# Weights in four chunks and a new instruction order in a fused scan and MLP kernel

## The chip, the core and the metric

The kernel runs on one core of a Trainium2 chip. Times are device microseconds of one execution; the figure for a kernel is the median over its runs.

## What is computed

The input is x, one sequence of 2,048 rows of 448 bf16 values. With xn the layernorm of x, the output is x + s * silu(m), where s is a complex diagonal state space model over the sequence and m a two-layer network for each row, which normalises xn again:

```
xn = layernorm(x)
s:  Bu = xn @ B_bar^T;  h[t] = Lam_bar * h[t-1] + Bu[t];  s = 2 Re(h @ C^T) + xn * Dskip
m:  layernorm(xn) @ w1 + b1  ->  gelu (tanh form)  ->  @ w2 + b2
out = x + s * silu(m)
```

w1 is 448 x 1792 and w2 1792 x 448, both bf16. B and C are 448 x 448, given as real and imaginary parts. The rest (Lambda, log_dt, Dskip, b1, b2) are vectors.

## The kernel before

**Tiling.** A block is 256 rows, laid out as 128 partitions with two rows each: `par` 0 is the even row and 1 the odd one. There are 8 blocks `x0` to `x7` and 4 groups `g` of two blocks. TensorE does nearly everything that is large; each part is one helper, and its line names it in the profile:

- `mm1` (L683) and, for group 0, `mm1_half` (L699) multiply the normalised and transposed rows `xn2T` by w1, two of the 14 column blocks of w1 a step (`j` from 0 to 6). `mm1_half` does it for one block of 256 rows at a time (`b` 0 or 1), so that work can begin with block 0 alone. ScalarE takes the gelu of each step from PSUM into `gT` (L690, L706).
- `mm2` (L714) multiplies `gT` by w2, 14 matmuls of 448 columns for each quarter of a group. VectorE adds b2 (L717, tile `b2bc`, which holds b2 on every partition), ScalarE takes a tanh (`th`, L718), VectorE forms `g_sb` (L719).
- `bu` (L613) multiplies the rows `xnT` by the transposed input matrix `BT`, in four steps a group (7 to 14 matmuls each), all into PSUM bank 4. ScalarE copies the bank into `u_sb` (L617) before the next step of `bu` may write it. `ssm` then scans along the sequence on VectorE (L638).
- `m0` (L602) and `ym` (L746, L749, L752) form the output of the state space model, with `CQ`, `CZ` and `M0` derived from C. VectorE multiplies it by `g_sb` (L755, tile t3) and adds the residual (L758), and SP stores it.
- `skip` (L730, L731) forms, for the odd rows, `xd` = xn * dbc and then `xr` = x + xd * g_sb. `dbc` is half of Dskip on every partition. It is loaded from POOL's queue and scaled by 0.5 on POOL (L338).

**Transposes and loads.** Nearly all DMAs are issued from SP's queue, in order: first x0 in two halves, w1, x1, b1 (one row of the w1 tile), B (tile `Bn`), w2, blocks 2 and 3, and C (tile `Cn`, which lies inside `gT`). Then come transposing DMAs: `xnT`, `xn2T` (for all groups but 0, whose `xn2T` comes from TensorE transposes, L379 and L437, copied by VectorE at L381 and L443), seven `BT`, each made from a `Bn` column block that VectorE finishes at L566, and four `Cr` that read all of C. `bu` step i needs BT i and 3 + i; its last step needs BT 6.

**Order.** Nothing is scheduled at run time. The helpers record 625 tasks, each with an engine, the keys it reads and the keys it writes. `emit` issues them in the order of a written list, `ORDER`. A task that the list `SECOND` names takes the second of two engines that it was given (`kb.either`). Each engine takes its instructions in that order and waits on semaphores for what a task's keys require, so an instruction that waits holds everything behind it on its engine, and a DMA that waits holds the queue.

**Chunks before.** w1 is loaded as two halves of 896 columns. Each half takes two DMAs, one for 384 of the 448 rows and one for the last 64, and a step waits for the halves that its columns lie in. w2 is loaded as two DMAs of 7 column blocks each, and `mm2` waits for both. The function `fcol` picks the columns of w1 so that block fi of a half is every seventh column, which fits the layout in which w2 is read (7 rows of w2 in a row for each partition).

Of the kernel before, what the change touches and what calls it, by code (L numbers as in the profile page):

```python
# [139 lines left out]
def dram_ap(t, offset, ap):  # L140
    return bass.AP(tensor=t.tensor, offset=offset, ap=ap)
# [4 lines left out]
ORDER = [int(k) for k in """  # L146
0 11 18 22 12 1 9 10 19 23 14 83 16 20 24 17 2 15 5 21 25 13 27 3 26 7 8 85 6 28 4 86 29 91 40 87 30 92 84 88 93 31 89 41 94 32 43 42 44 90 48 97 95
45 33 49 47 96 50 34 59 99 108 46 51 100 110 57 109 101 102 98 35 103 52 112 58 111 53 114 113 39 137 104 116 115 105 176 140 136 106 60 117 138 55 61
118 56 139 107 177 54 141 62 120 175 146 63 119 148 67 163 64 122 142 164 65 144 68 121 161 124 69 66 147 123 71 149 126 77 150 125 81 70 152 143 128
78 154 72 74 127 153 130 73 151 129 79 36 162 132 131 303 82 155 134 75 302 76 178 266 80 307 133 305 135 309 165 167 304 145 308 306 168 310 270 179  # L150
267 156 166 171 181 169 157 172 274 180 158 170 37 314 311 315 271 316 159 312 227 160 313 278 268 38 183 272 269 282 228 275 173 273 182 285 229 317
279 318 186 174 283 280 362 230 281 184 392 320 284 231 363 321 188 286 276 364 185 232 287 277 235 319 233 365 236 366 187 234 395 237 322 368 245
367 241 189 191 243 370 369 244 192 193 323 240 371 194 195 372 197 413 324 415 374 419 417 373 196 199 200 325 375 412 416 414 203 380 418 198 420
326 204 201 238 215 239 327 202 246 213 216 205 248 421 422 328 376 424 425 219 430 206 220 255 223 256 431 257 329 214 258 259 207 381 330 224 388
377 382 208 427 383 378 242 428 379 249 247 209 250 426 389 251 252 217 253 390 384 218 254 423 210 260 221 261 222 211 262 225 472 332 212 226 474
263 473 264 385 265 331 386 288 475 333 338 476 336 334 341 478 477 289 335 342 480 479 339 340 344 482 387 337 481 391 345 291 346 343 290 347 348
349 484 350 483 292 429 293 351 393 295 352 485 356 502 357 394 294 490 296 190 358 353 354 355 359 360 297 298 491 492 486 299 361 432 523 522 526
527 525 398 487 529 488 524 528 489 433 530 399 493 494 300 434 396 505 400 397 531 534 535 401 495 536 532 496 540 435 402 541 403 405 503 404 436
497 504 537 301 538 437 406 539 600 408 438 407 441 439 542 442 498 440 533 443 446 543 450 447 449 570 544 451 448 545 571 499 455 456 444 457 453
445 458 572 452 459 460 409 546 467 574 461 573 410 462 463 466 464 454 465 547 468 575 469 576 411 470 548 471 500 552 578 577 551 553 549 579 556  # L160
580 550 561 558 582 581 554 555 559 508 501 583 562 560 564 584 557 509 563 510 506 603 511 566 585 588 512 586 513 587 507 565 515 567 568 592 589
514 569 590 516 517 591 596 593 601 594 602 595 518 597 598 609 519 599 606 520 610 521 604 611 613 605 607 608 612 617 614 621 615 618 616 619 622
620 623 624
""".split()]
SECOND = [int(k) for k in """
138 141 142 143 167 171 173 197 199 217 223 284 311 318 320 393 395 396 421 422 424 425 428 503 505 506 507 532 534 535 538 541 603
""".split()]
# [11 lines left out]
def bass_recurrent_scan__ssm_conv_s5__mixer_channel_mlp__prompt_kernel(  # L179
# [18 lines left out]
    with ExitStack() as es:  # L198
# [75 lines left out]
        with nc.Block():  # L274
# [37 lines left out]

            NW1 = 2

            def ldw1(c, prio):
                w = F // NW1
                ld("sp", w1_sb[:, 0:3, c * w:(c + 1) * w],
                   dram_ap(B_w1, c * w, [[F, 128], [128 * F, 3], [1, w]]), [f"w1_{c}"], 384 * w * 2, prio, dur=0.55)
                ld("sp", w1_sb[0:64, 3, c * w:(c + 1) * w], dram_ap(B_w1, 384 * F + c * w, [[F, 64], [1, w]]),
                   [f"w1r_{c}"], 64 * w * 2, prio)  # L320

# [5 lines left out]
            ld("sp", w1_sb[64:65, 3, :], dram_ap(B_b1, 0, [[F, 1], [1, F]]), ["w1b"], 4000, S1 + 1)  # L327
            ldw1(1, S1 + 3)
            for ri, bm in enumerate((A_B_re, A_B_im)):
                ld("sp", Bn[:, ri * 3:ri * 3 + 3, D:896], dram_ap(bm, 0, [[D, 128], [128 * D, 3], [1, D]]),  # L330
                   [f"Bn{ri}"], 344000, S1 + 5, dur=0.9)
                ld("sp", Bn[ri * 64:ri * 64 + 64, 6, D:896], dram_ap(bm, 384 * D, [[D, 64], [1, D]]), [f"Bn6{ri}"], 57000, S1 + 5, dur=0.55)
            for q in range(2):
                ld("sp", w2_sb[:, q * 7:q * 7 + 7, :],
                   dram_ap(B_w2, q * 7 * 128 * D, [[7 * D, 128], [D, 7], [1, D]]), [f"w2_{q}"], 650000, S1 + 6, dur=1.7)
            ld("pool", b2bc[:], dram_ap(B_b2, 0, [[0, 128], [1, D]]), ["b2bc"], 114688, -50, reads=["sgn3"])
            ld("pool", dbc[:], dram_ap(A_Dskip, 0, [[0, 128], [1, D]]), ["dbc"], 114688, -20, reads=["b2bc"])
            pool(lambda e: e.tensor_scalar(dbc[:], dbc[:], 0.5, None, op0=ALU.mult), ["dbc"], ["dbc"], 0.8, -20)  # L338
            ldx(2, 2, S1 + 7)
# [334 lines left out]
            def fcol(fi):  # L674

                q, t = divmod(fi, 7)
                return slice(q * 896 + t, q * 896 + 896, 7)

            def mm1(g, j, prio):
                gx, gb = g % 2, g % 2  # L680
                b0 = (j % 2) * 2
                rhs = xn2T[:, gx, :, :].rearrange("p (r d) c -> p d r c", r=2)
                fns = [lambda e, k=k, d=d: e.matmul(psum[:, b0 + k, :], w1_sb[:, d, fcol(2 * j + k)],  # L683
                                                    rhs[:, d, :, :], start=(d == 0), stop=(d == 3))
                       for k in range(2) for d in range(4)]
                w = F // NW1
                cs = sorted({(2 * j * 128) // w, ((2 * j + 2) * 128 - 1) // w})
                pe(fns, [f"xmT{gx}_{b}" for b in range(2)] + [f"w1_{c}" for c in cs] + [f"w1r_{c}" for c in cs] + ["w1b"],
                   [f"ps{b0}", f"ps{b0 + 1}"], 1.75, prio)
                act(lambda e: e.activation(gT[:, gb, 2 * j:2 * j + 2, :], psum[:, b0:b0 + 2, :], ACT.Gelu_apprx_tanh),  # L690
                    [f"ps{b0}", f"ps{b0 + 1}"] + (WK + WKP if g == 1 else []), [f"gT{gb}_{2 * j + k}_{b}" for k in range(2) for b in range(2)], 1.05, prio - 70, "gelu")

            def mm1_half(j, b, k3, prio):
# [8 lines left out]
                       for k in range(2) for d in range(4)]  # L702
                w = F // NW1
                ws = sorted({(2 * j * 128) // w, ((2 * j + 2) * 128 - 1) // w})
                pe(fns, (["xmT0p0", "xmT0p1"] if b == 0 else ["xmT0_1"]) + [f"w1_{c}" for c in ws] + [f"w1r_{c}" for c in ws] + ["w1b"], [f"ps{k}" for k in banks], 0.89, prio)
# [4 lines left out]
            def mm2(g, b, par, prio):  # L710
                gb, q = g % 2, par * 2 + b
                n = (2 * g + b) * 2 + par
                gs, fb, bk = n % 8, n % 2, 5 + n % 2
                fns = [lambda e, fi=fi: e.matmul(psum[:, bk, 0:D], gT[:, gb, fi, q * 128:(q + 1) * 128], w2_sb[:, fi, :],  # L714
                                                 start=(fi == 0), stop=(fi == NF - 1)) for fi in range(NF)]
                pe(fns, [f"gT{gb}_{fi}_{b}" for fi in range(NF)] + ["w2_0", "w2_1"], [f"ps{bk}"], 2.66, prio)
                dve(lambda e: e.tensor_tensor(o2[:, fb, :], psum[:, bk, 0:D], b2bc[:], ALU.add), [f"ps{bk}", "b2bc"], [f"oo{fb}"], 0.62, prio - 76)  # L717
                act(lambda e: e.activation(th[:, fb, :], o2[:, fb, :], ACT.Tanh, scale=0.5), [f"oo{fb}"] + (WK + WKP if g == 0 else []), [f"th{fb}"], 0.58, prio - 75, "gelu")  # L718
                dve(lambda e: e.scalar_tensor_tensor(out=g_sb[:, gs, :], in0=th[:, fb, :], scalar=1.0, in1=o2[:, fb, :],  # L719
                                                     op0=ALU.add, op1=ALU.mult), [f"oo{fb}", f"th{fb}"], [f"g{gs}"], 0.6, prio - 60)  # L720
# [12 lines left out]
            def ym(g, b, par, prio):  # L733
# [9 lines left out]
                def part(c0, c1):  # L743
# [7 lines left out]
                    else:  # L751
# [5 lines left out]
                    res = xr[:, b, c0:c1] if par else x_all[:, 2 * g + b, 0, c0:c1]  # L757
                    dve(lambda e: e.tensor_tensor(o_sb[:, ob, par * D + c0:par * D + c1], t3[:, fb, c0:c1], res, ALU.add),  # L758
                        [f"t3{fb}_{c0}", f"t3{fb}_256"] + ([f"xr{b}"] if par else xk(2 * g + b)), [f"o{ob}_{par}_{c0}"], 0.1 + (0.28, 0.47)[par] * w / D, prio)
                    if last:  # L760
# [103 lines left out]
```

## Time and profile before

| | before |
|---|---|
| median of 13 runs | 161.78 us (161.08 to 164.58) |
| the profiled execution: time | 163.15 us |
| its span | 161.3 us |
| granted TensorE clock | full speed in all slices |
| TensorE busy | 151.1 us, 944 matmuls |
| VectorE, ScalarE, POOL busy | 132.7, 92.5, 56.4 us |
| DMA moved | 14.70 MB, 91 GB/s in the mean |

How to read it: a line of a group, of a timeline or of a wait names the engine, the line of the kernel and the tile written. PE is TensorE, PEld its weight loads, DVE is VectorE, ACT ScalarE, SP the engine that issues DMAs, and SPq its queue. In a timeline the first two columns are the start and the length in us, and brackets hold the idle time of the engine before the first of the instructions and what ended it. A line of waits has the total in us, the number and the longest.

### The profile page before, as it was taken

What the parts mean: (1) busy time and instruction counts of PE and PEld (TensorE: products, weight loads), DVE (VectorE), ACT (ScalarE), POOL (GpSimd) and SP (SyncE); (2) the same over time, 40 slices, a digit from 0 to 9 for tenths busy, and PEclk for the clock granted to TensorE, in tenths of its full rate; (3) what the DMA queues carried; (4) which work ended last, traced back from release to release, by engine and by line L of the source; (5) the groups of instructions that cost most, each with busy time, mean ns of one, the idle gap of its engine ahead of it and who ended that gap; (6) DMA issues with size and microseconds to landing.
All of it is one profiled execution on the core that took longest, in us unless ns stands there. A gap on an engine that the chain in (4) does not pass through costs nothing.

```text
span 161.3 us, 2700 instructions
## 1 busy us (share of the span) xinstructions
PE 151.1 (94%) x944; PEld 97.3 (60%) x944; DVE 132.7 (82%) x254; ACT 92.5 (57%) x152; POOL 56.4 (35%) x132
## 2 busy tenths in 40 slices
PE   6759999996999999999999999999999999999990
PEld 6559975664567665555565555567676665555560
DVE  5477998439799899699993999997999899896763
ACT  3757999948986894956369311343269678111100
POOL 5568928078400253210003752823046000005230
PEclk9999999999999999999999999999999999999999
DMA  4999999995882006000000802053601000010021
GB/s 95 307 303 383 273 211 182 113 195 110 155 142 100 0 0 120 14 0 0 0 0 0 228 8 55 0 145 91 122 4 57 0 4 0 0 57 0 21 92 59
DMA packets 29926, 14.70 MB, mean 91 GB/s; under 512 B 24597, under 2 KB 29593, under 8 KB 29914
## 3 DMA queue, kind: packets, MB, share of 16 engines
q1 hardware_dynamic: 29810, 14.31, 38.9%
q0 software_dynamic: 96, 0.23, 1.0%
q8 instruction: 7, 0.11, 0.3%
q14 instruction: 5, 0.04, 0.1%
q10 hardware_dynamic: 8, 0.00, 0.0%
HBM read 6.89 MB, written 1.84 MB: 54 GB/s over the span
## 4 chain that ended last, share of the span: by engine, by line
PE 73%; DVE 8%; issue 5%; DMA 5%; POOL 4%; ACT 2%; SPq 2%; POOLq 0%; DVEq 0%; ACTq 0%
PE psum L683 20%; PE psum L714 20%; PE psum L613 12%; PE psum L746 11%; DMA w_sb<-in_B_w_dram 5%; PE psum L749 4%; PE psum L602 3%; SPq L84 2%; DVE lnst L357 1%; PE psum L699 1%; POOL lnw L400 1%; DVE s_f L539 1%; POOL dbc L338 1%; DVE t L755 1%; PE psum L752 1%
## 5 line engine op out<-in xcount | busy, mean ns | idle before, releaser
L714 PE MATMUL psum<-w_sb,gT 128*128 128x448 bf16 x224 | 44.5, 352 | 0.0
L683 PE MATMUL psum<-xn2T,w_sb 128*128 128x512 bf16 x168 | 38.1, 379 | 0.0
L714 PEld LDWEIGHTS psum<-w_sb,gT 128*128 128x128 bf16 x224 | 21.8, 98 | 19.4
L683 PEld LDWEIGHTS psum<-xn2T,w_sb 128*128 128x128 bf16 x168 | 21.8, 132 | 12.9 <-issue 0.2
L690 ACT ACTIVATE gT<-psum 128x1024 bf16<-128x1024 f32 x21 | 21.5, 1023 | 11.8 <-PE psum L683 11.5
L613 PE MATMUL psum<-xnT,BT 128*128 128x256 bf16 x196 | 24.0, 273 | 1.8 <-ACT u_sb L617 1.8
L613 PEld LDWEIGHTS psum<-xnT,BT 128*128 128x128 bf16 x196 | 19.0, 98 | 7.2 <-issue 2.0
L718 ACT ACTIVATE th<-o 128x448 f32<-128x448 f32 x16 | 9.1, 573 | 20.7 <-DVE o L717 20.6
L699 PE MATMUL psum<-xn2T,w_sb 128*128 128x256 bf16 x112 | 12.8, 273 | 2.9 <-DMA w_sb<-in_B_w_dram 2.9
L719 DVE SCALAR_TENSOR_TENSOR g_sb<-th,o 128x448 bf16<-128x448 f32 x16 | 10.9, 682 | 4.7 <-ACT th L718 4.7
L755 DVE TENSOR_TENSOR t<-psum,g_sb 128x448 bf16<-128x448 f32 (+2 forms) x17 | 10.1, 591 | 5.6 <-PE psum L752 3.9
L638 DVE TENSOR_TENSOR_SCAN s_f<-cw,cur,v_sb 128x256 f32<-128x256 f32 x21 | 14.4, 735 | 0.2
L699 PEld LDWEIGHTS psum<-xn2T,w_sb 128*128 128x128 bf16 x112 | 12.1, 132 | 3.2 <-DMA w_sb<-in_B_w_dram 2.0
L730 POOL TENSOR_TENSOR xr<-xd,g_sb 128x448 f32<-128x448 bf16 x4 | 4.5, 1119 | 24.8 <-DVE g_sb L719 20.9
L421 DVE TENSOR_SCALAR xn_sb<-x_all,lnw 128x448 bf16<-128x448 bf16 x20 | 10.3, 534 | 2.6 <-POOL xd L730 2.4
L746 PE MATMUL psum<-CZ,h_sb 128*128 128x448 bf16 x56 | 11.9, 352 | 0.0
L717 DVE TENSOR_TENSOR o<-psum,b2bc 128x448 f32<-128x448 f32 x16 | 9.9, 618 | 2.4 <-PE psum L714 2.2
L617 ACT ACTIVATE u_sb<-psum 128x512 bf16<-128x512 f32 x12 | 7.1, 592 | 6.8 <-PE psum L613 6.8
L422 ACT ACTIVATE xn_sb<-x_all,lnw 128x448 bf16<-128x448 bf16 x10 | 7.5, 753 | 5.4 <-DVE xn_sb L421 4.6
L746 PE MATMUL psum<-CQ,h_sb 128*128 128x448 bf16 (+2 forms) x54 | 10.5, 332 | 0.0
L706 ACT ACTIVATE gT<-psum 128x512 bf16<-128x512 f32 x14 | 8.1, 594 | 3.8 <-PE psum L699 3.8
L357 DVE BATCH_NORM_STATS2 lnst<-x_all 128x6 f32<-128x448 bf16 x14 | 8.2, 610 | 1.8 <-DMA x_all<-in_A_x_dram 1.8
(154 smaller groups left out, 221.1 us busy)
## 6 DMA issues: line engine op xcount, KB each, us to landing
w_sb<-in_B_w_dram SPq DMA_DIRECT2D x2, 784.0 KB, 8.9
out_dram<-tmp SPq DMA_DIRECT2D x7, 224.0 KB, 2.0
w_sb<-in_B_w_dram SPq DMA_DIRECT2D x2, 672.0 KB, 6.3
x_all<-in_A_x_dram SPq DMA_DIRECT2D x3, 448.0 KB, 3.8
gT<-in_A_C_re_dram SPq DMA_DIRECT2D x1, 392.0 KB, 11.6
Bn<-in_A_B_re_dram SPq DMA_DIRECT2D x1, 336.0 KB, 8.0
Bn<-in_A_B_im_dram SPq DMA_DIRECT2D x1, 336.0 KB, 7.9
gT<-in_A_C_im_dram SPq DMA_DIRECT2D x1, 336.0 KB, 12.0
```

Of the source, the lines that this page charges most:

```text
L357: dve([lambda e, b=b, par=par, q=q: e.bn_stats(lnst[:, q, :], x_all[:, 2 * g + b, par, :])], [f"x{2 * g + b}"] + (["xmT0p1"] if (g, b) == ...
L421: on = [("dve", lambda e: e.tensor_scalar(dst, src, rs, nb, op0=ALU.mult, op1=ALU.add), 0.4, 0.12), ("act", lambda e: e.activation(dst, sr ...
L613: fns = [lambda e, r=r, m=m, d=d: e.matmul(psum[:, 4, r * NK:(r + 1) * NK], BT[:, m, d, :], xnT[:, gx, d, :], start=(d == 0), stop=(d == 6 ...
L638: dve(lambda e, i=i, ri=ri, init=init: e.tensor_tensor_scan(s_f[:, i, ri, :], col(R2, i).to_broadcast([128, NK]), v_sb[:, i, ri, :], init, ...
L683: fns = [lambda e, k=k, d=d: e.matmul(psum[:, b0 + k, :], w1_sb[:, d, fcol(2 * j + k)], rhs[:, d, :, :], start=(d == 0), stop=(d == 3)) fo ...
L690: act(lambda e: e.activation(gT[:, gb, 2 * j:2 * j + 2, :], psum[:, b0:b0 + 2, :], ACT.Gelu_apprx_tanh), [f"ps{b0}", f"ps{b0 + 1}"] + (WK ...
L699: fns = [lambda e, k=k, d=d: e.matmul(psum[:, banks[k], :].rearrange("p (r c) -> p r c", r=2)[:, :, cs], w1_sb[:, d, fcol(2 * j + k)], rhs ...
L714: fns = [lambda e, fi=fi: e.matmul(psum[:, bk, 0:D], gT[:, gb, fi, q * 128:(q + 1) * 128], w2_sb[:, fi, :], start=(fi == 0), stop=(fi == N ...
L717: dve(lambda e: e.tensor_tensor(o2[:, fb, :], psum[:, bk, 0:D], b2bc[:], ALU.add), [f"ps{bk}", "b2bc"], [f"oo{fb}"], 0.62, prio - 76)
L719: dve(lambda e: e.scalar_tensor_tensor(out=g_sb[:, gs, :], in0=th[:, fb, :], scalar=1.0, in1=o2[:, fb, :], op0=ALU.add, op1=ALU.mult), [f" ...
L746: fns = [lambda e, k=k: e.matmul(psum[:, bk, c0:c1], h_sb[:, hb, k, k0:k0 + 128], cm[:, k, c0:c1], start=(k == 0), stop=False) for k in ra ...
L755: dve(lambda e: e.tensor_tensor(t3[:, fb, c0:c1], psum[:, bk, c0:c1], g_sb[:, gs, c0:c1], ALU.mult), [f"ps{bk}", f"g{gs}"], [f"t3{fb}_{c0} ...
```

## The change

**Chunks.** w1 and w2 are cut into chunks of 4, 4, 4 and 2 column blocks (`CH`). w1 takes eight DMAs instead of four, on SP's queue, and w2 four instead of two. A row of a chunk of w1 is 1,024 bytes (512 in the last one) where it was 1,792; a partition's piece of w2 is 3,584 bytes (1,792 in the last) where it was 6,272. A step of `mm1` or `mm1_half` waits for one chunk alone, `mm2` for all four of w2. x1 still stands between the first piece of w1 and the next.

**Engines.** The scaling of dbc may be on ScalarE or VectorE instead of POOL; the new list puts it on VectorE. The last two output additions (odd rows of the last block, 256 and 192 columns) may be on VectorE or POOL; the list puts the one of 192 columns on POOL. These two no longer need each other's product.

**Order.** Both lists are new; there are 631 tasks. Of what moves: TensorE does six half blocks for block 0 before the transposes of block 1, where it did five, and one after them. In group 1 it does two steps of `mm1` where it did one between the second and third step of `bu`, and three where it did one before the last. SP issues the 64-column piece of C's imaginary part behind two xnT, four BT and the two xn2T of group 1, where it stood ahead of them all; then two BT, the four Cr, and only then the last BT. POOL loads b2bc ahead of its arithmetic on the parameters instead of behind it. VectorE does the first `xd`, and takes the statistics of blocks 2 and 3 before it finishes the second BT's input. On ScalarE the second copy of u_sb comes after four tanh and before the last xn_sb pieces of that stretch, where it came after three tanh and an xn_sb. At the end TensorE does the 192 columns before the 256.

```diff
 ORDER = [int(k) for k in """
...
 SECOND = [int(k) for k in """
...
-            NW1 = 2
+            CH = ((0, 4), (4, 4), (8, 4), (12, 2))
+            chunk = [c for c, (_, n) in enumerate(CH) for _ in range(n)]
 
             def ldw1(c, prio):
-                w = F // NW1
-                ld("sp", w1_sb[:, 0:3, c * w:(c + 1) * w],
-                   dram_ap(B_w1, c * w, [[F, 128], [128 * F, 3], [1, w]]), [f"w1_{c}"], 384 * w * 2, prio, dur=0.55)
-                ld("sp", w1_sb[0:64, 3, c * w:(c + 1) * w], dram_ap(B_w1, 384 * F + c * w, [[F, 64], [1, w]]),
-                   [f"w1r_{c}"], 64 * w * 2, prio)
+                a, w = CH[c][0] * 128, CH[c][1] * 128
+                ld("sp", w1_sb[:, 0:3, a:a + w], dram_ap(B_w1, a, [[F, 128], [128 * F, 3], [1, w]]), [f"w1_{c}"], 384 * w * 2, prio, dur=0.55)
+                ld("sp", w1_sb[0:64, 3, a:a + w], dram_ap(B_w1, 384 * F + a, [[F, 64], [1, w]]), [f"w1r_{c}"], 64 * w * 2, prio)
...
             ldw1(0, S1 + 1)
             ldx(1, 1, S1 + 2)
             ld("sp", w1_sb[64:65, 3, :], dram_ap(B_b1, 0, [[F, 1], [1, F]]), ["w1b"], 4000, S1 + 1)
-            ldw1(1, S1 + 3)
+            for c in (1, 2, 3):
+                ldw1(c, S1 + 3)
...
-            for q in range(2):
-                ld("sp", w2_sb[:, q * 7:q * 7 + 7, :],
-                   dram_ap(B_w2, q * 7 * 128 * D, [[7 * D, 128], [D, 7], [1, D]]), [f"w2_{q}"], 650000, S1 + 6, dur=1.7)
+            for c, (a, n) in enumerate(CH):
+                ld("sp", w2_sb[:, a:a + n, :], dram_ap(B_w2, a * 128 * D, [[n * D, 128], [D, n], [1, D]]), [f"w2_{c}"], 98000 * n, S1 + 6, dur=0.5 + 0.1 * n)
...
-            pool(lambda e: e.tensor_scalar(dbc[:], dbc[:], 0.5, None, op0=ALU.mult), ["dbc"], ["dbc"], 0.8, -20)
+            kb.either(("act", lambda e: e.activation(dbc[:], dbc[:], ACT.Copy, scale=0.5), 0.6, 0.2),
+                      ("dve", lambda e: e.tensor_scalar(dbc[:], dbc[:], 0.5, None, op0=ALU.mult), 0.2, 0.12), ["dbc"], ["dbc"], -20)
...
             def fcol(fi):
 
-                q, t = divmod(fi, 7)
-                return slice(q * 896 + t, q * 896 + 896, 7)
+                a, n = CH[chunk[fi]]
+                return slice(a * 128 + fi - a, (a + n) * 128, n)
...
-                w = F // NW1
-                cs = sorted({(2 * j * 128) // w, ((2 * j + 2) * 128 - 1) // w})
+                cs = [chunk[2 * j]]
...
-                pe(fns, [f"gT{gb}_{fi}_{b}" for fi in range(NF)] + ["w2_0", "w2_1"], [f"ps{bk}"], 2.66, prio)
+                pe(fns, [f"gT{gb}_{fi}_{b}" for fi in range(NF)] + [f"w2_{c}" for c in range(4)], [f"ps{bk}"], 2.66, prio)
...
-                    dve(lambda e: e.tensor_tensor(o_sb[:, ob, par * D + c0:par * D + c1], t3[:, fb, c0:c1], res, ALU.add),
-                        [f"t3{fb}_{c0}", f"t3{fb}_256"] + ([f"xr{b}"] if par else xk(2 * g + b)), [f"o{ob}_{par}_{c0}"], 0.1 + (0.28, 0.47)[par] * w / D, prio)
+                    add = lambda e: e.tensor_tensor(o_sb[:, ob, par * D + c0:par * D + c1], t3[:, fb, c0:c1], res, ALU.add)
+                    rd = [f"t3{fb}_{c0}", f"t3{fb}_256"] if c0 == 0 and not (last and par) else [f"t3{fb}_{c0}"]
+                    rd += [f"xr{b}"] if par else xk(2 * g + b)
+                    on = [("dve", add, 0.1 + (0.28, 0.47)[par] * w / D, 0.12), ("pool", add, 0.2 + 1.1 * w / D, 0.15)]
+                    if last and par:
+                        kb.either(*on, rd, [f"o{ob}_{par}_{c0}"], prio)
+                    else:
+                        dve(add, rd, [f"o{ob}_{par}_{c0}"], on[0][2], prio)
```

## The prediction

> **What bounds the kernel now.** I read the page first: busy shares, the DMA row of the slices, the chain by engine.
>
> ```profile
> PE 151.1 (94%) x944; PEld 97.3 (60%) x944; DVE 132.7 (82%) x254; ACT 92.5 (57%) x152; POOL 56.4 (35%) x132
> DMA  4999999995882006000000802053601000010021
> PE 73%; DVE 8%; issue 5%; DMA 5%; POOL 4%; ACT 2%; SPq 2%; POOLq 0%; DVEq 0%; ACTq 0%
> ```
>
> TensorE is busy 151.1 of 161.3 us. The change leaves its 944 matmuls as they are, so it can only win from the 10.2 us in which TensorE stands, and can only lose by adding to them. The DMA engines are full over the first tenths of the span (4 us a slice), idle for long stretches later. The list of waits says where TensorE stands:
>
> ```profile
> PE psum L699 <- DMA w_sb<-in_B_w_dram: 2.9, 2, 1.8
> PE psum L613 <- ACT u_sb L617: 1.8, 2, 1.4
> PE psum L777 <- POOL ident L278: 1.4, 1, 1.4
> ```
>
> Two waits for w1, two for ScalarE's copy of a PSUM bank, the start. The rest is the tail (last matmul 157.27, span 161.3). TensorE's timeline places them:
>
> ```profile
> 7.33 2.80 PE L699 MATMUL psum<-xn2T,w_sb 128*128 128x256 bf16 x24 [1.13 <-DMA w_sb<-in_B_w_dram]
> 11.89 1.93 PE L699 MATMUL psum<-xn2T,w_sb 128*128 128x256 bf16 x16 [1.75 <-DMA w_sb<-in_B_w_dram]
> ...
> 35.61 1.89 PE L683 MATMUL psum<-xn2T,w_sb 128*128 128x512 bf16 x8
> 38.95 1.69 PE L613 MATMUL psum<-xnT,BT 128*128 128x256 bf16 x14 [1.45 <-ACT u_sb L617]
> ...
> 42.69 0.94 PE L613 MATMUL psum<-xnT,BT 128*128 128x256 bf16 x7 [0.32 <-ACT u_sb L617]
> ```
>
> Behind 43 us it never stands again until the tail. So all that the change can move lies before 43 us and behind 157.
>
> **1. The start: 0.45 us won.** The first w1 matmul waits for the whole first half of w1. The DMA view of that stretch (KB, us from issue to landing) shows what follows it in the queue:
>
> ```profile
> w_sb<-in_B_w_dram SPq DMA_DIRECT2D x1, 672.0 KB, 7.4
> x_all<-in_A_x_dram SPq DMA_DIRECT2D x1, 224.0 KB, 5.2
> w_sb<-in_B_w_dram SPq DMA_DIRECT2D x1, 112.0 KB, 7.5
> ```
>
> By issue plus this time: x0 is there at 3.3, the first half (784 KB) at 7.2, x1 at 8.5, the second half at 11.7. That is 201 KB/us for the first half, and 224 for the 1008 KB behind it. A new chunk of four columns is 448 KB; at 201 it lands 2.2 us behind x0, at 5.5. Then xn2T ends last: its copies (L381) end at 6.77. TensorE starts near 6.87 instead of 7.33: 0.45 won (nothing, if the chunk lands no sooner than now).
>
> **2. The second wait: 0.9 us won.** By bytes alone x1 lands at 6.5, chunks 1, 2 and 3 at 8.5, 10.5 and 11.5. The rows of a chunk are 1,024 bytes (512 in the last), not 1,792. In the trace's packets 1,792 bytes take some 78 ns and 896 bytes 47; on the line through both, 1,024 take 52 and 512 take 34, 1.17 and 1.5 times as long a byte (an estimate). Then it is 5.9, then 6.9 for x1, and 9.3, 11.6 and 13.1. The new order runs 48 matmuls of 109 ns (six half blocks, two a chunk) before x1's transposes. It wants chunk 1 at 6.87 + 1.75 = 8.6 and chunk 2 at 10.4 or 1.75 behind the late chunk 1. Waits: 0.1 by bytes, 0.7 + 0.55 by packets. b2bc, now loaded from POOL's queue in this very stretch (112 KB, 0.5 us at that rate), may add its share; its 0.8 us on POOL lies in the 2.1 us that POOL waits for ScalarE's cw. I take 0.85 against 1.75; bounds 0.1 and 1.9. x1's own chain (8.56 to 13.55 now, 5.0 us) is ready at 11.5 to 12, before its place at 13: hidden, spare 1 us. w2's four pieces land some 1 us later than now (17.95) and are wanted at 20.6 instead of 21.96: hidden, spare 1.5.
>
> [...]
>
> **3. The wait for u_sb: 1.8 us won.** The chain of waits goes back from 38.95 to POOL:
>
> ```profile
> 27.24 0.64 POOL L84 DMA_DIRECT2D dbc<-in_A_Dskip_dram  x1
> 33.14 1.57 POOL L338 TENSOR_SCALAR dbc<-dbc 128x448 bf16<-128x448 bf16 x1 [5.26 <-DMA dbc<-in_A_Dskip_dram]
> 34.80 2.02 POOL L730 TENSOR_TENSOR xd<-xn_sb,dbc 128x448 bf16<-128x448 bf16 x2
> ```
>
> xd holds xn_sb until 35.84, VectorE's next xn_sb (L421) waits 2.4 us for that, ScalarE's xn_sb waits 3.07 for VectorE, and the copy of u_sb stands behind it in ScalarE's queue. In the new order VectorE scales dbc (the nearest row, L421, has 0.39 us for the same shape), VectorE does the first xd, and ScalarE's u_sb copy stands ahead of that xn_sb. All 1.77 us go. VectorE is not the bound at that point, but the price moves to it: it now stands if dbc lands late. dbc lands near 33.1 now; VectorE comes to it near 35, spare 1.5 to 2.
>
> **4. What is late next: 1.3 us lost.** TensorE arrives 1.35 us earlier (steps 1 and 2) at what comes by DMA. L683 needs both xn2T of the second group. Now it starts at 35.61, and the second landed at 29.82 + 5.6 = 35.4: no spare.
>
> ```profile
> xn2T<-xn_sb SPq DMA_TRANSPOSE x2, 5.5
> 28.54 4.32 SPq L83 DMA_TRANSPOSE xn2T<-xn_sb  x2
> ```
>
> (DMA view of that stretch, then SP's queue, where the second issue alone took 3.0 us.) Issue to landing was 5.5 us for these two, 3.1 for later ones; the slow pair ran beside dbc's load (28.8 to 32). In the new order they again follow two xnT and four BT. x2 and x3 land some 1 us later behind the smaller pieces, and VectorE takes their statistics before it ends the second BT's input, so the pair is issued some 0.6 us later than now, at 29.2 and 30.5. At 3.1 us they land at 33.6, TensorE wants them at 34.3: no wait. At 5.5 they land at 36: 1.7 us. The BT behind bu's second step, issued between, has the same two cases: 0, or up to 1.1 more. Bounds 0 and 2.8; dbc is still loaded at the same place, so I take nearly half, 1.3. Behind it SP has a 56 KB piece of C_im, two BT, four Cr and the last BT, some 10 us at 1.3 us each: the last BT lands near 43.5 to 45, and is wanted at 34.3 + 3.45 + 1.53 + 5.18 = 44.5 plus what was waited: no more than 0.5, within the bounds.
>
> **5. The tail: 0.25 us won.**
>
> ```profile
> 157.91 0.36 DVE L755 TENSOR_TENSOR t<-psum,g_sb 128x192 bf16<-128x192 f32 x1
> 158.30 0.36 DVE L758 TENSOR_TENSOR tmp<-t,xr 128x192 bf16<-128x192 bf16 x1
> ```
>
> Now VectorE ends 1.39 us behind the last matmul, with six operations in a row. In the new order the 192 columns come first and their addition goes to POOL; behind the last matmul stand one t and one addition of 256 columns (0.41 + 0.42 in the rows): 0.9. That wins 0.45. SP ends on 28 final waits instead of 25, at 0.065 us each: 0.2 lost.
>
> **Sum.** 161.3 - 0.45 - 0.9 - 1.8 + 1.3 - 0.25 = 159.2 of span. The profiled execution took 163.15 in all, 1.85 around its span; the median of the 13 runs, 161.78, is 1.4 below it. I take the same 2.1 us off the median: 159.7.
>
> **Rivals.** (a) dbc does not hurt the transposes, step 4 costs nothing: 158.4. For it: later transposes land in 3.1 us, and b2bc's load at 23 us slowed nothing. Against: dbc and its neighbours keep their places. (b) The wait moves: step 4 costs its 2.8, or w1 still comes as late as now; the gain of steps 1 and 2 is given back and 161.1 remains. For it: L683 has no spare now. (c) Slower: the C_im piece is now issued behind the xn2T pair, all four Cr wait for it, and the last BT stands behind them in SP's queue. Its landing took 11.7 us from issue, in a full queue. If that holds it lands at 43.5, the last BT 8.5 us later at 52, TensorE stands 7.5 us at bu's last step, and the time is 165.9. It decides once the piece takes over some 8 us (spare 1 beyond the 3.5 that the order allows, then the gain of 3.4); the queue is nearly empty by then and x2-size loads later land in 3.8, so it is unlikely. (d) The chunks bring nothing because small rows load slower: 160.6, inside the forecast's range.
>
> **How the numbers follow.** Forecast (own range 158.9 to 160.9) 0.43; (a) 0.22; (b) 0.19; (c), with any other new stall, 0.16. A measurement of this kernel can tell 0.5%, 0.8 us, from no change: limits 161.0 and 162.6. The forecast and (a) are faster; (b) lies at the limit and gives 0.04 to faster, 0.15 to same; (c)'s weak half gives 0.04 to same, the rest slower. Faster 0.69, same 0.19, slower 0.12. The range goes from 158.2, (a) with a little of step 2's lower bound, to 162.2, which is (b) with steps 2 and 4 both near their upper bounds; some 0.1 is left out on either side.
>
> **What would show it.** L699 standing on DMA once near 6.9 for xn2T and 0.1 to 1.3 us in all for w1; no wait on u_sb near 38; a wait for BT or xn2T of 0 to 2.8 us between 32 and 37; VectorE ending 0.9 us behind the last matmul. Wrong would be: a wait for w1 over 1.9, VectorE standing on dbc near 35, the last BT landing behind 46, or any wait of TensorE behind 46 us.

## The result and the profile after

The changed kernel takes 165.43 us (median of 11 runs, 164.09 to 166.0), the kernel before 161.77 in the same comparison: a ratio of 1.0233, 95% interval 1.0207 to 1.0259. It is 3.7 us slower where 2.1 us less were forecast.

The profiled execution of it took 163.41 us, less than any timed one. The timed ones list a mean granted TensorE clock of 0.984 to 0.994 in all but one (which took 165.28 us at 1.0), the profiled one 0.997. So this profile shows where the waits are, and understates them. From its page, the busy shares, the DMA row and the chain by engine:

```profile
PE 152.3 (94%) x944; PEld 94.3 (58%) x944; DVE 135.6 (84%) x252; ACT 94.3 (58%) x154; POOL 56.5 (35%) x132
DMA  4999997999784003510000312506210000010013
PE 63%; DVE 15%; DMA 10%; SPq 7%; issue 2%; ACT 2%; DVEq 0%
```

TensorE stands for 9.3 us in all, where it stood for 10.2, but DMA's share of the chain has doubled from 5 to 10%, and VectorE's from 8 to 15%: the middle stage now hangs on x2 and x3, then their statistics on VectorE, then the transposes. The list of TensorE's waits, and its timeline:

```profile
PE psum L699 <- DMA w_sb<-in_B_w_dram: 1.5, 1, 1.5
...
PE psum L614 <- DMA BT<-Bn: 1.4, 1, 1.4
PE psum L699 <- issue: 0.6, 1, 0.6
PE psum L614 <- ACT u_sb L618: 0.2, 1, 0.2
```

```profile
7.60 1.91 PE L699 MATMUL psum<-xn2T,w_sb 128*128 128x256 bf16 x16 [0.56 <-issue]
11.00 3.69 PE L699 MATMUL psum<-xn2T,w_sb 128*128 128x256 bf16 x32 [1.49 <-DMA w_sb<-in_B_w_dram]
...
31.66 1.69 PE L614 MATMUL psum<-xnT,BT 128*128 128x256 bf16 x14 [1.41 <-DMA BT<-Bn]
```

The wait for u_sb near 38 is gone, as forecast. The wait for w1 is still 1.5, and a new one of 1.4 for B's transpose has come. The DMA view of the first 22 us shows what is late (KB, us from issue to landing):

```profile
q0 software_dynamic: 48, 0.11, 4.7%
...
x_all<-in_A_x_dram SPq DMA_DIRECT2D x1, 224.0 KB, 5.9
...
b2bc<-in_B_b_dram POOLq DMA_DIRECT2D x1, 112.0 KB, 6.0
```

x1 takes 5.9 us where it took 5.2, though the pieces ahead of it are smaller and the first of them lands at 5.6, as forecast. x1 lands at 9.2, not 6.5 to 6.9, and x2 and x3 at 23.3 where they came at 20.1. Besides the smaller pieces, the one thing new in that stretch is b2's broadcast load on GpSimd's queue (the software queue), which the new order issues at 3.4 us instead of 18.4. In the trace's packet records its 16 packets of 4,480 bytes ran between 6.1 and 8.7 us and took 0.17 to 1.49 us each. In the kernel before they ran at 23.0 us, behind the last load of the first stream (landed at 22.9), and took 0.17 us each.

The tail of VectorE:

```profile
157.70 0.41 DVE L754 TENSOR_TENSOR t<-psum,g_sb 128x256 bf16<-128x256 f32 x1
158.15 0.42 DVE L757 TENSOR_TENSOR tmp<-t,xr 128x256 bf16<-128x256 bf16 x1
```

VectorE ends 0.96 behind the last matmul (157.61), as forecast, but the span ends 3.0 behind VectorE where it ended 2.7 behind.

### The profile page after: what moved, and what is told of

It reads as the page before. It is cut to its first block, busy times and chain, and to the rows that moved or that the text cites. A ratio compares the mean times of both kernels' runs of the same rounds, so it can differ in the third digit from the quotient of the medians.

```text
span 161.6 us, 2714 instructions
## 1 busy us (share of the span) xinstructions
PE 152.3 (94%) x944; PEld 94.3 (58%) x944; DVE 135.6 (84%) x252; ACT 94.3 (58%) x154; POOL 56.5 (35%) x132
## 3 DMA queue, kind: packets, MB, share of 16 engines
HBM read 6.89 MB, written 1.84 MB: 54 GB/s over the span
## 4 chain that ended last, share of the span: by engine, by line
PE 63%; DVE 15%; DMA 10%; SPq 7%; issue 2%; ACT 2%; DVEq 0%
PE psum L713 21%; PE psum L684 16%; PE psum L614 11%; PE psum L745 8%; DMA x_all<-in_A_x_dram 7%; SPq L84 7%; PE psum L603 3%; DVE s_f L639 3%; DMA BT<-Bn 3%; PE psum L748 2%; DVE tmp L757 2%; DVE t L754 2%; DVE lnst L358 1%; DVE pa L631 1%; DVE pb L632 1%
## 5 line engine op out<-in xcount | busy, mean ns | idle before, releaser
L684 PEld LDWEIGHTS psum<-xn2T,w_sb 128*128 128x128 bf16 x168 | 18.7, 112 | 15.7
L729 POOL TENSOR_TENSOR xr<-x_all,xr 128x448 f32<-128x448 bf16 x8 | 10.2, 1275 | 34.7 <-DVE xr L730 21.5
L639 DVE TENSOR_TENSOR_SCAN s_f<-cw,cur,v_sb 128x256 f32<-128x256 f32 x21 | 16.1, 799 | 0.4
L699 PEld LDWEIGHTS psum<-xn2T,w_sb 128*128 128x128 bf16 x112 | 11.8, 112 | 2.9 <-DMA w_sb<-in_B_w_dram 1.8
L423 ACT ACTIVATE xn_sb<-x_all,lnw 128x448 bf16<-128x448 bf16 x14 | 10.3, 753 | 3.0 <-issue 1.5
L718 DVE SCALAR_TENSOR_TENSOR g_sb<-th,o 128x448 bf16<-128x448 f32 x16 | 9.8, 617 | 1.2 <-ACT th L717 1.0
L729 POOL TENSOR_TENSOR xd<-xn_sb,dbc 128x448 bf16<-128x448 bf16 x5 | 6.5, 1290 | 7.3 <-DVE xr L730 6.9
```

The source lines that it names most:

```text
L423: ("act", lambda e: e.activation(dst, src, ACT.Identity, bias=nb, scale=rs), 0.75, 0.2)]
L639: dve(lambda e, i=i, ri=ri, init=init: e.tensor_tensor_scan(s_f[:, i, ri, :], col(R2, i).to_broadcast([128, NK]), v_sb[:, i, ri, :], init, ...
L699: fns = [lambda e, k=k, d=d: e.matmul(psum[:, banks[k], :].rearrange("p (r c) -> p r c", r=2)[:, :, cs], w1_sb[:, d, fcol(2 * j + k)], rhs ...
L729: kb.either(("pool", lambda e, o=o, i0=i0, i1=i1, op=op: e.tensor_tensor(o, i0, i1, op), 1.37, 0.15), ("dve", lambda e, o=o, i0=i0, i1=i1, ...
```

## The experiments

Theories at the start: *broadcast* (b2's early load on GpSimd's queue slows the whole first stream of loads), *chunks* (more and smaller pieces load slower), *clock* (the lower granted clock of the timed runs is a loss of its own). Medians:

| kernel | us | before, beside it | ratio (95%) |
|---|---|---|---|
| after_again | 164.79 | 161.65 | 1.017 (1.010 to 1.024) |
| b2bc_late | 162.19 | 161.65 | 1.004 (1.000 to 1.007) |
| b2bc_early | 165.09 | 161.65 | 1.022 (1.017 to 1.026) |
| halves | 165.24 | 161.65 | 1.020 (1.013 to 1.026) |
| before_again | 161.63 | 162.08 | 0.999 (0.995 to 1.003) |
| b2bc_sp | 162.30 | 162.08 | 1.003 (0.999 to 1.007) |
| chunks_alone | 163.62 | 162.08 | 1.012 (1.002 to 1.022) |
| both_sp | 161.73 | 162.08 | 0.999 (0.995 to 1.003) |
| filler | 162.77 | 161.64 | 1.008 (1.005 to 1.011) |
| final_waits | 160.61 | 161.64 | 0.993 (0.991 to 0.996) |
| best_pieces | 159.91 | 161.64 | 0.990 (0.986 to 0.994) |
| best_two | 159.97 | 161.64 | 0.990 (0.988 to 0.992) |

**A second profile of the changed kernel** (after_again, no edit).

> The changed kernel, unaltered: a second profile of it. The first profiled execution took 163.41 us, less than any of its eleven timed ones (median 165.43), and its granted clock came up 2.1 us later than in the profile of before (6.93 instead of 4.79 us). If the clock is part of the loss (clock theory), this one has a mean granted clock of 0.985 to 0.99 and a span near 163.6, and its waits for DMAs are those of the first profile (1.5 for w1, 1.4 for BT). If the loss is only in the waits, the clock is again 0.997 or more and the waits are about 2 us longer than in the first profile.

```profile
PE psum L614 <- ACT th L717: 2.0, 1, 2.0
PE psum L699 <- DMA w_sb<-in_B_w_dram: 2.0, 1, 2.0
...
PE psum L684 <- DMA xn2T<-xn_sb: 0.6, 1, 0.6
```

The waits were longer, and the profiled execution, at 165.02, was 1.6 longer than the first at the same clock (0.998). The first of these lines names a tanh, but the BT that this step of `bu` needs landed at 36.68 and the step began at 36.77: it is the wait for B's transpose again. So waits alone can give a time of 165. In its timed executions the clock was 0.988, 0.995 and 0.989. Both expectations were half right: either kind of execution occurs.

**b2's load, late again** (b2bc_late) and, in the kernel before, **early** (b2bc_early). Task numbers of ORDER; 42 and 36 are b2's load.

```diff
 changed kernel
-91 14 28 42 4 92 97 ...    168 85 88 137
+91 14 28 4 92 97 ...       168 85 42 88 137
 kernel before
-43 42 44 90 ...            79 36 162
+43 42 36 44 90 ...         79 162
```

> The changed kernel with one DMA moved back: the broadcast load of b2 is issued on GpSimd's queue behind the parameter arithmetic, near 23 us as in the kernel before, not at 3.4 us. Broadcast theory (its packets slow the whole first stream by about 2 us): the second x block lands near 7 instead of 9.2, TensorE's wait for w1 falls from 1.5 to 0 to 0.5 us, x2 and x3 land 1.5 to 2 us earlier, the wait for BT falls from 1.4 to under 0.5, and the time falls by 2 to 3 us, to 162.5 to 163.5. Chunk theory (the loads are slow because they are in more and smaller pieces): landings move by under 0.5 us and the time stays at 165 to 165.5. Clock theory: the waits may shrink, but the clock stays near 0.985 and most of the loss stays, 164 to 165.

> The kernel before with one DMA moved: the broadcast load of b2 goes out on GpSimd's queue at about 3.4 us, as in the changed kernel, all else as before. Broadcast theory: the second x block lands 1.5 to 2 us later (10 instead of 8.6), TensorE's wait for the second w1 piece grows from 1.75 to 3 to 3.7 us, and the time rises by 1.5 to 2.5 us, to 163.3 to 164.3. Chunk theory and clock theory: the time stays within 0.5 us of 161.8.

One DMA's place, and nothing else, takes 2.6 us off the changed kernel (164.79 to 162.19) and puts 3.4 us on the kernel before (161.65 to 165.09). The landings moved as the broadcast theory has them: with the load late x1 came at 7.9, x2 and x3 at 21.6; with it early in the kernel before, x1 at 9.75 and x2 and x3 at 22.1. The lines of x1, first of b2bc_late, then of b2bc_early (5.9 in the changed kernel, 5.2 in the kernel before):

```profile
x_all<-in_A_x_dram SPq DMA_DIRECT2D x1, 224.0 KB, 4.6
...
x_all<-in_A_x_dram SPq DMA_DIRECT2D x1, 224.0 KB, 6.5
```

In the packet records, 713 packets of 1,024 bytes ran between 6.0 and 8.5 us with the load late, 278 in the changed kernel. With the load late, TensorE's waits are:

```profile
PE psum L713 <- DVE o L716: 1.5, 1, 1.5
...
PE psum L699 <- DMA w_sb<-in_B_w_dram: 0.6, 1, 0.6
```

and VectorE's list says what the first one is:

```profile
DVE o L716 <- DMA b2bc<-in_B_b_dram: 1.8, 1, 1.8
```

At its late place the load takes 6.8 us, to 26.75, and VectorE's first add of b2 now stands on it. In the kernel before it had landed at 24.1.

The rise in b2bc_early was larger than expected, though its w1 wait grew only from 1.75 to 2.4. Its timeline and its stretches (length, busy time, number of matmuls, granted clock, DMA share, GB/s) show the rest:

```profile
13.17 3.36 PE L699 MATMUL psum<-xn2T,w_sb 128*128 128x256 bf16 x16 [2.40 <-DMA w_sb<-in_B_w_dram]
```

```profile
11.00:13.00 2.00, 0.00 (x0) 1.00 1.12 296
13.00:14.00 1.00, 0.83 (x6) 0.74 1.10 350
14.00:16.00 2.00, 2.00 (x11) 0.50 1.03 398
16.00:20.00 4.00, 4.00 (x39) 0.89 1.06 320
```

TensorE idles for 2.4 us, and behind that its clock is 0.5 for some 3.4 us: by the windows 0.26 + 1.0 + 0.44 = 1.7 us of it is lost. The same 16 matmuls took 1.93 in the profile of before and 3.36 here.

**Halves in the changed order** (halves).

```diff
-CH = ((0, 4), (4, 4), (8, 4), (12, 2))
+CH = ((0, 7), (7, 7))
```

> The changed kernel with w1 and w2 in two halves again, all other instructions in the changed order, the early broadcast of b2 too. Chunk theory: the loads are quicker again, x2 and x3 land 1 us or more earlier, and the time falls by 1 to 2 us, to 163.5 to 164.5. Broadcast theory: the four pieces are worth what the prediction gave them, up to 0.9 us at the w1 wait and 0.45 at the first matmul, so halves are 0.5 to 1.5 us slower, 166 to 167.

Neither: 165.24, no difference from four pieces that these four runs can show. Both effects are there, with opposite signs. x2 and x3 land 1.2 us earlier (22.1), as the chunk theory has it, and the wait for w1 is 3.15 instead of 1.5 to 2.0, with the clock at 0.5 behind it again, as the broadcast theory has it:

```profile
13.53 4.47 PE L699 MATMUL psum<-xn2T,w_sb 128*128 128x256 bf16 x24 [3.15 <-DMA w_sb<-in_B_w_dram]
```

**A second profile of the kernel before** (before_again, no edit).

> The kernel before, unaltered: a second profile of it. The profile that the prediction was made from took 163.15 us, 1.4 over the median, though its granted clock was 1.0. Theory: one of the waits that the prediction wanted to win (1.13 and 1.75 for w1, 1.45 and 0.32 for u_sb) is some 1.4 us shorter in a usual execution, and the span here is 159.5 to 160.2; then that part of the forecast gain was never there. Rival: the waits are the same within 0.3 us each and the first profile's extra time lay elsewhere; then the forecast gain was all there to be had.

It took 161.00 us, span 159.2. Its timeline:

```profile
11.12 1.93 PE L699 MATMUL psum<-xn2T,w_sb 128*128 128x256 bf16 x16 [0.92 <-DMA w_sb<-in_B_w_dram]
...
34.84 1.94 PE L683 MATMUL psum<-xn2T,w_sb 128*128 128x512 bf16 x8
36.82 1.69 PE L613 MATMUL psum<-xnT,BT 128*128 128x256 bf16 x14
```

The second w1 wait is 0.92, not 1.75, and the wait of 1.45 for u_sb is not there at all: dbc landed at 30.8, not at 33.05. These two, 0.83 and 1.45 us shorter, cover the 2.15 us between the two executions. They are most of what the prediction meant to win, and a median execution, 0.65 to 1.1 above this one, can hold less than half of them.

**Four pieces alone, in the old order** (chunks_alone).

```diff
 kernel before
-NW1 = 2
+CH = ((0, 4), (4, 4), (8, 4), (12, 2))
-... ["w2_0", "w2_1"]
+... [f"w2_{c}" for c in range(4)]
 ORDER: the new w1 and w2 pieces right behind the last old one
```

> The kernel before with only w1 and w2 in four pieces instead of two; every other instruction keeps its place, b2's load stays late on GpSimd's queue. By the prediction's steps 1 and 2 the first matmul on w1 starts 0.45 us earlier and the second wait for w1 falls from 1.75 to 0.85: 1.35 us won, 160.4. Rival (more and smaller pieces are slower to load, so that the last of w1, w2 and the x blocks behind them land later): no gain, 161.5 to 162.5, with x2 and x3 landing 1 us or more later than the 20.1 of before.

Slower, by 1.5 (four runs, 162.0 to 164.1). The first matmul starts at 7.11, 0.2 us earlier and not 0.45, the w1 wait is 0.17, better than forecast, and at 20.2 TensorE is 1 us ahead of before_again. Then it loses that again (its lines are numbered one lower):

```profile
33.27 1.69 PE L612 MATMUL psum<-xnT,BT 128*128 128x256 bf16 x14 [0.78 <-DMA BT<-Bn]
...
38.63 1.69 PE L612 MATMUL psum<-xnT,BT 128*128 128x256 bf16 x14 [1.47 <-ACT u_sb L616]
```

w2 lands at 18.6 instead of 17.1 to 17.95, and x2 and x3 at 20.4 instead of 19.2 to 20.1. The packets agree: by the medians of the trace records one of 512 bytes took 36 ns, of 1,024 bytes 46, of 1,792 bytes 74, of 3,584 (w2 in four) 146, of 6,272 (w2 in halves, before_again) 247. By these, w1's 1.6 MB over 16 engines take 4.1 us in halves and 4.9 in four pieces, w2's 4.0 and 4.1 (an estimate from the packets). But the two waits shown are not the pieces' alone: the BT of the first was issued at 26.8 and landed at 33.1, beside D's load on GpSimd's queue (27.4 to 33.1), and dbc at 33.1 comes with the same wait for u_sb in the profile of before. Neither wait is in before_again. How the 1.5 us divide between the smaller pieces and D's load is open.

**b2's load on SyncE's queue** (b2bc_sp), then **D's too** (both_sp).

```diff
-ld("pool", b2bc[:], ..., 114688, -50, reads=["sgn3"])
+ld("sp", b2bc[:], ..., 114688, -50)                      (behind x2 and x3)
-ld("pool", dbc[:], ..., 114688, -20, reads=["b2bc"])     (both_sp alone)
+ld("sp", dbc[:], ..., 114688, -20)                       (behind C's first loads)
```

> The changed kernel with the broadcast load of b2 on SyncE's queue, right behind the load of x2 and x3, not on GpSimd's. With that load issued late on GpSimd's queue it took 6.8 us to land (19.9 to 26.8) and TensorE lost 1.5 us behind VectorE's add of b2. Broadcast theory (a transfer of GpSimd's queue is itself slow and slows all others while it runs): here it lands by 23.5 to 24.5, that wait is gone, nothing else moves by more than 0.5 us, and the time is 160.3 to 161.0. Rival (something else is late right behind it: the transposes that now start 0.5 us later): a wait of 0.8 us or more for BT or xnT, and 161.5 to 162.2.

> As the one before, and the broadcast load of D goes on SyncE's queue too, behind the loads of C, so that GpSimd's queue carries nothing in the first 45 us. In the changed kernel that load ran from 29.6 to 33.6, across the transposes that feed B-bar's and x's matmuls. If it slows them as b2's slows the loads, the last two of the first four B transposes and the xn2 transposes land 0.7 to 1.5 us earlier; since TensorE waits for them in some executions (1.4 and 2.0 us in the two profiles of the changed kernel), the time is 0.3 to 1 us below the run with b2's load alone on SyncE's queue. Rival: the transposes are ahead of TensorE by then, and the two are within 0.3 us of one another.

On SyncE's queue b2's load cost 0.57 us (x2 and x3 at 20.87, b2 at 21.44), and the wait for b2 was gone. So was the one for w1, but in this profile for another reason too: by the trace's clock records the clock came up only at 10.86 us, so that the 48 matmuls ahead of x1's transposes took 6.97 us and not 5.6, and w1 was there in time. Yet b2bc_sp gained nothing on b2bc_late by the medians (162.30 and 162.19): the rival was right. A BT and the xn2T pair were late instead, the second xn2T at 36.9, with D's load landing at 32.4 beside them. With D's load moved as well the pair landed at 35.2, and the median fell by 0.6, as the theory of that run had it, though the spreads of the two overlap (160.7 to 163.0 and 160.3 to 162.8). TensorE stands there still:

```profile
35.33 3.62 PE L684 MATMUL psum<-xn2T,w_sb 128*128 128x512 bf16 x16 [0.54 <-DMA xn2T<-xn_sb]
```

That is 0.5 us behind the same point of before_again (34.84), which TensorE reached without a wait, the same pair having landed at 34.80. Ahead of both lie x2 and x3, their statistics, and a row of transposes issued 1.3 us apart on SyncE, so before_again had nothing to spare there, and both_sp lost in this stage what it had won ahead of it (`mm2` began at 20.34, in before_again at 21.19).

**Matmuls in the w1 wait** (filler).

```diff
+pe([lambda e: e.matmul(psum[:, 7, 0:128], ident[:, :], ident[:, :], start=True, stop=True)
+    for _ in range(20)], ["ident"], ["ps7", "fill"], 1.2, ...)      (ahead of the third half block)
```

> The changed kernel with 20 matmuls of ident by ident (128 columns each, into a PSUM bank that nothing else uses then) put on TensorE between the matmuls of w1's first piece and those of its second, that is into its wait for w1. They add about 1.1 us of TensorE work to a wait of 1.5 to 2.5 us and change no result. Two runs with a wait of 2.4 and 3.15 us there had the granted clock at 0.5 for some 2 us behind it, and lost 1.6 to 1.9 us more than the wait; with waits of 1.5 and 2.0 us it stayed at 1.0. Clock theory (the usual execution of the changed kernel has a wait over 2 us, and the idle time itself brings the clock down): the time falls by 1.2 to 2.2 us, to 163.2 to 164.2, and the mean granted clock is 0.995 or more. Rival (the clock falls for another reason, as the loads' own power): the clock stays at 0.985 to 0.99 and the time at 165.0 to 166.5.

```profile
8.72 1.28 PE L785 MATMUL psum<-ident 128*128 128x128 bf16 x20
11.85 3.68 PE L699 MATMUL psum<-xn2T,w_sb 128*128 128x256 bf16 x32 [1.84 <-DMA w_sb<-in_B_w_dram]
```

20 matmuls more, and 162.77 instead of 164.8 to 165.4. w1 comes as late as ever (TensorE does nothing of the kernel's own from 8.8 to 11.85 here), but the clock stays at 1.0 behind the wait, and the mean clocks are 0.995 to 1.0. This is what the clock theory asks for: one such stretch at half clock cost 1.7 us in b2bc_early. But it is not separated from the waits. The profile of filler shows no wait in the middle stage, where the two of the unaltered kernel show 1.4 and 2.6, and executions of that kernel at a clock of 0.997 to 1.0 took 163.4, 165.0 and 165.3. How much of the 2.0 to 2.7 us is the clock stays open. (A mean of 0.988 does not give it either: the 0.997 of the profile after is a clock that fell at 160.5, when TensorE was done.)

**Final waits, and two versions with all that was learnt** (final_waits; best_pieces; best_two).

```diff
 emit(), all three
+late = [t for t in order if t.eng == "sp"][-5]
 for t in order:
+    if t is late:
+        for sem, val in self.counts.items():
+            if val and sem not in ENGS and seen.get(sem, 0) < val:
+                eng.wait_ge(self.sems[sem], val); seen[sem] = val
 both_sp's loads for the last two; best_two alone
-CH = ((0, 4), (4, 4), (8, 4), (12, 2))
+CH = ((0, 6), (6, 8))
```

> The kernel before with SyncE's 28 final waits for DMAs long landed moved ahead of its fifth-last output DMA, where SyncE is idle; only those for the last outputs stay at the end. In the trace of before the span ends 1.15 us behind the landing of the last output, twelve waits of 0.06 us each later. Theory: 0.5 to 0.8 us faster than before, 160.9 to 161.2. Rival (the end is set by the landing and by what follows the last wait, not by the number of waits): within 0.2 us of 161.7.

> The changed kernel with both broadcasts on SyncE's queue and SyncE's final waits for old DMAs ahead of its fifth-last output. The version with the broadcasts alone took 161.73, with 22 waits of 0.06 us behind the last output's landing. Theory: 0.5 to 0.9 us less, 160.8 to 161.2. Rival: as for the waits in the kernel before, no gain, 161.5 to 161.9.

> As the one before, but w1 and w2 in two pieces of 6 and 8 of the 14 column tiles, not in four: rows of 1,536 and 2,048 bytes for w1 where four pieces have 1,024 and, in the last, 512. In the traces a 512-byte packet took 38 ns, one of 1,024 bytes 50 to 58 and one of 1,792 bytes 77, so that w1 should take about 1.2 us less of the queue, and all behind it, x2 and x3 too, should land that much earlier: x2 and x3 by 19.5 to 20.2 instead of 21.2, xn2T by 34.2 instead of 35.2. TensorE then waits up to 1 us for the second w1 piece where it waited 0.2. Theory (x2 and x3 are what the middle stage waits for): 0.2 to 0.8 us less than with four pieces, 160.2 to 160.9. Rival (the w1 wait gives it all back): 161.0 to 161.5.

The waits alone win 1.0 us (interval of the ratio 0.991 to 0.996), somewhat more than expected: in its trace the span ends 0.31 behind the last landing, before it was 1.15. On both_sp the gain was larger still, 1.4 us (each taken against the kernel before beside it). best_pieces and best_two are both faster than the kernel before by 1.7 us, 1.0%, and equal to one another: two pieces win nothing over four, though both are 1 us below the time that the rival gave. The timeline of best_pieces (its lines are numbered six higher):

```profile
9.03 3.69 PE L705 MATMUL psum<-xn2T,w_sb 128*128 128x256 bf16 x32 [0.23 <-DMA w_sb<-in_B_w_dram]
...
34.30 3.64 PE L690 MATMUL psum<-xn2T,w_sb 128*128 128x512 bf16 x16
```

best_two waits 1.8 for w1 instead and starts the same matmuls at 35.25. With the final waits in both, best_two against final_waits gives what the new order and the moved broadcasts are worth together: 0.6 us by the medians, which is not clear of noise (final_waits spreads from 159.1 to 161.3). Of the 1.7 us, 1.0 is the final waits.

## Why the prediction was wrong

**The step that failed is the term for b2bc in step 2** ("(112 KB, 0.5 us at that rate), may add its share"). Sized by bytes it was 0.5; moving the load cost 3.4 us in the kernel before, and in the changed kernel the late place was worth 2.6 and SyncE's queue 3.4 (3.66 above the kernel before beside it, then 0.22). It acts in three ways: x1 and w1 come 1 to 2 us later, so the wait goes past the 1.9 given as its upper bound (2.0 in the second profile, some 3 in filler); x2 and x3 come 2 us later, which adds to step 4; and the longer wait can bring the half clock, 1.7 us more in b2bc_early, which was in no bound. The rate itself came from loads on one queue; nothing in step 2 priced a load on a second queue beside them. Rival (a) read a row for that, b2's load at 23 us that "slowed nothing", but there it ran behind the last load of the stream. The row that spoke against it was shown too: the transposes that ran beside dbc's load took 5.5 us, not 3.1. That was weighed in step 4 and not in step 2.

**Second, the base of the sum.** All was taken off an execution 1.4 us above the median, and the result shifted by those 1.4. But the second profile shows that these were stalls which steps 2 and 3 meant to win, and that a faster execution does not have. That makes the forecast up to 1.4 us too low. It alone would have left the time at 161.1, within the range; b2's load took it out.

Point by point. Step 1 was right in mechanism: the first piece landed at 5.4 to 5.7, and TensorE started at 6.89 to 7.17 in four profiles without the early load (7.60 in the profile after, where the 16 short matmuls ahead took 2.1 us instead of 1.2, the clock coming up at 6.93 and not at 4.79). Step 2's packet estimates came close (52 and 34 ns forecast for 1,024 and 512 bytes, medians of 46 and 36 measured), with some luck: the 47 ns for 896 bytes that they rest on is what x0's packets took at the very start (mean 50), while B's packets of the same size, in the full stream, had a median of 55. Without the early load the wait was 0.2 to 0.6 (b2bc_sp aside), better than its 0.85, but against 0.92, not 1.75. Step 3 was right for the profiled execution but for 0.2 that stayed, and worth nothing for the wait of 1.45 in before_again, where it was not there. Step 4's 1.3 was met by 1.4 in the first profile, 2.6 in the second, 0.9 and 1.1 with b2's load on SyncE's queue, and nothing in best_pieces; x2 and x3, about 1 us later as forecast, stand ahead of these waits, but no run moved them alone. Step 5 had VectorE's 0.45 right and the waits wrong: not their number (28 for 25) but their place counts, since one for an output now comes early, and it and all behind it are 22, where they were 12. The tail won 0.1, not 0.25.

Of the rivals, (a) and (c) did not come: C_im's piece landed 2.6 us after its issue, and TensorE never stood behind 46 but for 0.2. The last BT did land behind 46, at 46.5, since all ahead of it was late, but TensorE came to it at 47.5. (b), the wait that moves, did come. (d) holds for chunks_alone in that the pieces brought nothing, and four pieces gave no gain over two with the broadcasts moved (159.91 and 159.97 us); the 1.5 us lost in chunks_alone are not in it. The slower side was reached by a mechanism that no rival named.

## What to carry to other kernels

Here a 112 KB load on GpSimd's queue, beside the first stream of loads, cost 2.6 to 3.4 us, not the 0.5 us of its bytes over the stream's rate. So do not price a load by its bytes alone: look at which queue issues it, what its packets took where such a load ran beside others, and put a small broadcast on the queue whose order you control (0.57 us in b2bc_sp). Ahead of any sum, take a second profile of the kernel as it is, and count as winnable only the stalls that both show. A wait of TensorE can cost more than itself, by the clock behind it (2.40 us of wait and 1.7 us more in b2bc_early); if the wait can't be removed, spare matmuls in it are cheap (in filler 20 of them took 1.28 us of it, and the clock stayed at 1.0).

## What the runs showed of the hardware

- The packets of a 112 KB broadcast on GpSimd's queue, beside SyncE's first stream of loads, were spread in after over 2.85 us (6.11 to 8.96), up to 1.49 us each, and between 6.0 and 8.5 us 278 packets of 1,024 bytes ran there where 713 ran in b2bc_late, without it. Behind the stream, in before, the same packets took at most 0.17 us each and 0.4 us in all. The time from issue to landing hides this: 6.0 us in after, 5.7 in before. On SyncE's queue the load cost 0.57 us (b2bc_sp). Why the packets took longer beside the stream was not tried.
- The granted clock fell to 0.5 behind idle times of 2.40 us (b2bc_early) and 3.15 us (halves), not behind 1.75 (before), 1.84 (filler) or 2.02 (after_again). By the windows it was at 0.5 from 13.48 to 16.88 us in b2bc_early and from 13.82 to 17.2 in halves, 3.4 us both times. In the 3.4 us ahead of its fall TensorE had been busy for 1.0 us in b2bc_early, for 0.3 in halves, and for 0.5 in after, where it fell at 160.53, behind the last matmul; around the 2.02 of after_again no stretch of 3.4 us held less than 1.4. What brings the clock down, and whether the place of a wait counts as well as its length, was not shown: no run shifted one to see.
- Ahead of the first clock record (4.8 us in before, 6.9 in after, 10.9 in b2bc_sp) the page's clock row shows full speed, yet matmuls ran at about half their pace: in before one of 128 columns every 107 ns, behind the record every 56.
- SyncE's waits on semaphores long reached took 0.06 us each and stand in the span when they are last: 12 of them in the kernel before, 22 in the changed one, and 1.0 us won by moving them in the first (final_waits, 160.61 for 161.64).
